# Six pairs' softmax reciprocals: one narrow transpose and two broadcast reads in place of six transposes

## The chip, the cores and the metric

The kernel runs on one core of a Trainium2 chip. What is measured is the device time of one execution in microseconds (us). TensorE (PE) does matmuls and transposes, VectorE (DVE), ScalarE (ACT) and GpSimd (POOL) the elementwise work, SyncE (SP) and GpSimd issue the transfers. SBUF is the on-chip memory of the operands, PSUM the one that TensorE writes its results to, DRAM the chip's large memory.

## The reference

Attention over keys that fall in the same hash bucket as the query (2 batches, 8 heads, 768 tokens, head size 64), and behind it two feed-forward blocks on the 1536 tokens, all in float32:

```python
def _attn_ref(q, k, v, proj):
    scale = 1.0 / np.sqrt(D)
    q_bits = (np.einsum('bhsd,dk->bhsk', q, proj) > 0).astype(np.int64)
    k_bits = (np.einsum('bhsd,dk->bhsk', k, proj) > 0).astype(np.int64)
    powers = 2 ** np.arange(n_bits)
    q_bucket = np.sum(q_bits * powers, axis=-1)
    k_bucket = np.sum(k_bits * powers, axis=-1)
    mask = q_bucket[:, :, :, None] == k_bucket[:, :, None, :]
    scores = scale * np.matmul(q, k.transpose(0, 1, 3, 2))
    scores = np.where(mask, scores, -1000000000.0)
    scores = scores - np.max(scores, axis=-1, keepdims=True)
    attn = np.exp(scores)
    attn = attn / (np.sum(attn, axis=-1, keepdims=True) + 1e-09)
    return np.matmul(attn, v).astype(np.float32)
...
    x = np.ascontiguousarray(attn_out.transpose(0, 2, 1, 3)).reshape(B * S, H * D)
    h = np.maximum(x @ w_in, 0.0)         # first block
    x = h * h @ w_out
    h = x @ w_in                          # second block, weights of its own
    g = h * (1.0 / (1.0 + np.exp(-h)))
    return (g @ w_out).astype(np.float32)
```

## The kernel before

The 16 heads (2 batches of 8) are worked on as 8 pairs. For each head the 768 queries are cut in two halves of 384, which gives 32 units (u), four to a pair, and each unit is cut into three blocks of 128 queries (j). The attention stage is one loop over steps, numbered d from -5 to 98, and a unit takes three steps. The order on every engine is that of the code: no scheduler moves anything in this stage. In an ordinary step TensorE transposes two blocks of the exponentials (transp, three 128x128 transposes into a tile t each, 384 of the tile's 512 columns), does the value matmuls of the two blocks of two steps ago (av, four matmuls into o) and the scores of the next query block (score_mm, four matmuls into one of two buffers s). ScalarE casts the two transposed tiles (t_hi, into th) and takes the exponential (score_exp, with the row sums into sums). VectorE takes the row maxima (row_max, row_live) and the rests of the casts (t_lo, into tl).

Six times, at the steps d = 17, 29, 41, 53, 65 and 77, and once before at d = 5, a step is long: bits_mm adds twelve narrow matmuls for the hash bits of the pair that comes next (into bs and bt), and VectorE compares them (bits_cmp). SP then copies the bits to where the next scores read them (place_bits).

The sums of a finished pair p are turned into factors in these steps. norm_sums (GpSimd) and norm_rows (VectorE reciprocal, into the same tile of 128x12) leave one reciprocal for each query in a column for each block and head. The unnormalised output ta (x_sum) has its queries along the free dimension, so the factors are needed along it as well: norm_rows lets GpSimd write each reciprocal 64 times (tile rw, 128 x 768), rb_mm has TensorE transpose that in six 128x128 blocks into a buffer s (named rb), x_norm has ScalarE copy it back to rw, and x_mul has GpSimd multiply ta by it into yf. x_put copies yf into the operand xk of the feed-forward blocks for the pairs below 6. The last pair (7) goes another way.

What a step does beside this stands in lists that are filled ahead of the loop: `todo` (at the end of a step), `mid` (behind row_live), `extra` (behind bits_mm). The first four tiles of the first w_in, given in 64-bit words, are made into float32 during attention: W_STEPS holds for each the steps of its load (w_load), its absolute value (w_abs on ScalarE and w_limit on GpSimd) and its three integer operations on VectorE (w_exp, w_sign, w_low). X_STEPS are the steps of four sums on GpSimd (x_form). The two feed-forward blocks come after attention and are put in order by a planner with costs of its own.

The lines that hold most of what is changed:

```python
            extra[k].append((rb_mm, x_norm, p))
            at(k + 1, x_mul, p)
            at(k + 1, x_put, p)
```

Of the kernel before, what the change touches and what calls it, by code (L numbers as in the profile page):

```python
# [11 lines left out]
F32 = mybir.dt.float32  # L12
# [9 lines left out]
B, H, S, D = 2, 8, 768, 64  # L22
NT, DM, FF = B * S, H * D, 2048
NB = 6
NPAIR = B * H // 2
NU = NPAIR * 4
QW = 384
# [10 lines left out]
W_LO = float(np.uint32(897 << 20).view(np.float32))  # L38
W_HI = float(np.uint32((1150 << 20) | 0xFFFFF).view(np.float32))
V_LAG = 4  # L40
W_STEPS = ((6, 10, 17, 17, 29), (8, 17, 29, 41, 41), (30, 41, 53, 53, 65), (44, 53, 65, 92, 93))
WA = 4
FB = 4
NP = FB // 2
# [129 lines left out]
    (10, (0, 0), (0, 3)),  # L174
)
NFORM = 4
X_STEPS = (82, 84, 86, 88)
FLIPPED = {2: ((0, 4, 1.0), (4, 6, -1.0)), 6: ((0, 6, -1.0),), 7: ((0, 2, 1.0), (2, 6, -1.0))}
FLIP = ({(1, 2), (2, 2), (2, 3)}, {(0, 2), (0, 3), (1, 3), (1, 0), (1, 1)})
MINUS = ({0: "-", 2: "-", 3: "-", 4: "r", 11: "r"}, {15: "-"})  # L180
# [519 lines left out]
def lsh_attention_moe_moe(ctx, tc, kd, qk, qf, fq, v, pc, wi1, wo1, wi2, wo2, out):  # L700
    nc = tc.nc
# [14 lines left out]
    att = ctx.enter_context(ExitStack())  # L716
    ac = att.enter_context(tc.tile_pool(name="ac", bufs=1))
    a1 = att.enter_context(tc.tile_pool(name="a1", bufs=1))
    a2 = att.enter_context(tc.tile_pool(name="a2", bufs=2))
    ps_s = att.enter_context(tc.tile_pool(name="ps_s", bufs=2, space=PSUM))  # L720
    ps_t = att.enter_context(tc.tile_pool(name="ps_t", bufs=3, space=PSUM))
    ps_o = att.enter_context(tc.tile_pool(name="ps_o", bufs=1, space=PSUM))

    ident = ac.tile([128, 128], F32, name="ident")
# [30 lines left out]
    def scale_q(p):  # L755
        q = pair[p]["r"][0]
        nc.scalar.mul(out=q, in_=q, mul=SCALE)
# [23 lines left out]
    def bits_mm(p):  # L781
        t = pair[p]
        hp, lp = t["hp"], t["lp"]
        ops = [(w[:, 48 * i : 48 * i + 48], x) for i in range(2) for (w, x) in ((pjh, hp[i]), (pjl, hp[i]), (pjh, lp[:, i]))]
        s = ps_s.tile([128, 2, 512], F32, tag="s", name=f"bs{p}")[:, 0], ps_t.tile([128, 512], F32, tag="t", name=f"bt{p}")
        for z in range(2):
            for j, (w, x) in enumerate(ops):
                mm(s[z][0:48, 0:QW], w, x[:, z * QW : (z + 1) * QW], start=j == 0, stop=j == 5)  # L788
        return s

    def bits_cmp(s, p, z):
        if z == 0:
            pair[p]["bt"] = a1.tile([128, S], F32R, tag="bt", name=f"bt{p}")
        nc.vector.tensor_scalar(
            out=pair[p]["bt"][0:48, z * QW : (z + 1) * QW],
            in0=s[z][0:48, 0:QW],
            scalar1=tm[0][0:48, 0:1],
            scalar2=tm[0][0:48, 1:2],
            op0=ALU.is_gt,
            op1=ALU.mult,  # L800
        )
# [173 lines left out]
    P, stats, otile, sums = {}, {}, {}, {}  # L975

    def warm_up(n):
        for _ in range(n):
            mm(warm, zb[:, 0:128], zb[:, 0:512], start=True, stop=True)
# [13 lines left out]
    def row_max(u, j, s):  # L993
        m = mt[:, (u * 3 + j) % 4]
        nc.vector.tensor_reduce(out=m[:, 0:1], in_=s[:, :, 0:QW], op=ALU.max, axis=AX.XY, negate=True)  # L995
        return m

    def row_live(m):
        nc.vector.tensor_scalar(out=m[:, 1:2], in0=m[:, 0:1], scalar1=LIM, scalar2=1.0, op0=ALU.is_lt, op1=ALU.mult)
        nc.vector.tensor_scalar(out=m[:, 2:3], in0=m[:, 0:1], scalar1=LIM, scalar2=m[:, 0:1], op0=ALU.is_lt, op1=ALU.mult)  # L1000

    def score_exp(u, j, s, m):
        p = u // 4
        if u % 4 == 0 and j == 0:
            sums[p] = a2.tile([128, 12], F32, tag="sums", name=f"sums{p}")
        e = P[u, j] = ac.tile([128, S], F32, tag="P", bufs=6, name=f"P{u}_{j}")
        c = (u % 4) * 3 + j
        nc.scalar.activation(  # L1008
            out=e.rearrange("p (a b) -> p a b", a=2),
            in_=s[:, :, 0:QW],  # L1010
            func=AF.Exp,
            scale=m[:, 1:2],
            bias=m[:, 2:3],
            accum_out=sums[p][:, c : c + 1],
        )

    PT = {}

    def transp(g, t=None):
        u, kt = divmod(g, KT)  # L1020
        if t is None:
            t = ps_t.tile([128, 512], F32, tag="t", name=f"t{g}")
        for j in range(3):
            nc.tensor.transpose(t[:, j * 128 : (j + 1) * 128], P[u, j][:, kt * 128 : (kt + 1) * 128], ident)  # L1024
        PT[g] = (t,)

    def t_hi(g):
        th = a1.tile([128, QW], F32R, tag="th", bufs=6, name=f"th{g}")
        nc.scalar.copy(out=th, in_=PT[g][0][:, 0:QW])  # L1029
        PT[g] += (th,)  # L1030

    def t_lo(g):
        t, th = PT[g]
        tl = a1.tile([128, QW], F32R, tag="tl", bufs=6, name=f"tl{g}")
        nc.vector.tensor_tensor(out=tl, in0=t[:, 0:QW], in1=th.bitcast(F32), op=ALU.subtract)  # L1035
        PT[g] = th, tl
# [31 lines left out]
    def norm_rows(p):  # L1068
        ri = sums[p]
        nc.vector.reciprocal(out=ri, in_=ri)  # L1070
        w = rows[p] = a1.tile([128, 6, 2, 64], F32, tag="rw", bufs=2, name=f"rw{p}")
        nc.gpsimd.tensor_copy(out=w, in_=ri.rearrange("p (h c) -> p c h", h=2).unsqueeze(3).broadcast_to([128, 6, 2, 64]))

    rows = {}

    def rb_mm(p):
# [38 lines left out]
    todo = defaultdict(list)  # L1115
    extra = defaultdict(list)
    mid = defaultdict(list)
    long, scale = {}, {}
    last = defaultdict(list)

    def at(g, fn, *a):
        todo[g].append((fn, a))

    for p in range(1, NPAIR):
        d0 = 12 * (p - 1)
# [18 lines left out]
    for p in range(NPAIR):  # L1144
        d0 = 12 * (p + 1)
        at(d0 + (-3 if p < NPAIR - 1 else -4), norm_sums, p)
        at(d0 + (2 if p < NPAIR - 1 else -3), norm_rows, p)
        at(d0 + (3 if p < NPAIR - 1 else 0), x_sum, p)
        if p < NPAIR - 1:
            k = d0 + (5 if p < NPAIR - 2 else 9)  # L1150
            extra[k].append((rb_mm, x_norm, p))
            at(k + 1, x_mul, p)
            at(k + 1, x_put, p)

    for k, d in enumerate(X_STEPS):
        at(d, x_form, k)
    for i, (d_load, d_abs, *d_dve) in enumerate(W_STEPS):
        key = (0, 0, i)
# [5 lines left out]
        d0 = d_dve[2]  # L1164
# [6 lines left out]
    with tc.manual_schedule():  # L1171
# [15 lines left out]
        c, k = slice(64, 64 + NBR), first["c"]  # L1187
        nc.vector.tensor_tensor(
            out=pdx, in0=k[:, 0:NBR].unsqueeze(1).broadcast_to([128, 2, NBR]), in1=k[:, NBR : 3 * NBR].rearrange("p (a b) -> p a b", a=2), op=ALU.mult
# [45 lines left out]
        for d in range(-5, G // 2 + 3):  # L1235
            ready, new = new, None
            g = 2 * d
            if ready:
                m = row_max(*ready)
            if 0 <= g - 1 < G and g - 1 not in early_lo:  # L1240
                t_lo(g - 1)
            if ready:
                row_live(m)
            for fn, a in mid.pop(d, []):
                fn(*a)
            if 0 <= g < G and d in (92, 94):
                t = ps_s.tile([128, 2, 512], F32, tag="s", name=f"t{g}")
                for i in range(2):
                    transp(g + i, t[:, i])
                t_hi(g)  # L1250
                t_hi(g + 1)
                t_lo(g)
            elif 0 <= g < G:
                transp(g)
                t_hi(g)
                t_lo(g)
                transp(g + 1)
                t_hi(g + 1)
            more = extra.pop(d, [])
            if ready and more and d not in long:  # L1260
                score_exp(*ready, m)
            if d in long:
                score_exp(*ready, m)
                if d in scale:
                    scale_q(scale.pop(d))
            for n in (g - V_LAG, g + 1 - V_LAG):
                if 0 <= n < G:
                    av(n)
            if d in long:
                t = bits_mm(long[d])  # L1270
            held = [(dve, pe(p), p) for pe, dve, p in more]
            if d in long:
                bits_cmp(t, long[d], 0)
                t_lo(g + 1)
                bits_cmp(t, long[d], 1)
            for dve, t, p in held:
                dve(t, p)
            if ready and not more and d not in long:
                score_exp(*ready, m)
            u, j = divmod(d + 5, 3)  # L1280
            if u < NU:
                new = u, j, score_mm(u, j)
            for fn, a in todo.pop(d, []) + last.pop(d, []):
                fn(*a)
            warm_up(WARM.get(d, 0))
        p = NPAIR - 1
        for z in (1, 0):
            t = ps_t.tile([128, 512], F32, tag="t", name=f"rb{p}_{z}")
# [12 lines left out]
        t = dict(yf=yf, xk=xk, wpa=wpa, raw=raws, wt=wt, pair=both, src=((wi1, wo1), (wi2, wo2)), out=out)  # L1301
# [58 lines left out]
```

## Time and profile before

| what | value |
|---|---|
| time, median of 3 runs | 724.61 us (724.58 to 725.61) |
| the profiled execution: its own time | 725.18 us |
| its span, first to last instruction | 723.40 us |
| TensorE busy | 718.1 us, 99% |
| VectorE busy | 609.6 us, 84% |
| ScalarE busy | 543.1 us, 75% |
| GpSimd busy | 263.0 us, 36% |
| granted TensorE clock over the span | 1.00 |

The profile is one execution. Its own time is longer than its span by what lies ahead of the first instruction and behind the last. Matmuls overlap each other, and their ends are modelled, so a busy TensorE is not one at its peak: the distance from one start to the next tells more than the durations.

### The profile page before, as it was taken

What the parts mean: (1) busy time and instruction counts of PE and PEld (TensorE: products, weight loads), DVE (VectorE), ACT (ScalarE), POOL (GpSimd) and SP (SyncE); (2) the same over time, 40 slices, a digit from 0 to 9 for tenths busy, and PEclk for the clock granted to TensorE, in tenths of its full rate; (3) what the DMA queues carried; (4) which work ended last, traced back from release to release, by engine and by line L of the source; (5) the groups of instructions that cost most, each with busy time, mean ns of one, the idle gap of its engine ahead of it and who ended that gap; (6) DMA issues with size and microseconds to landing.
All of it is one profiled execution on the core that took longest, in us unless ns stands there. A gap on an engine that the chain in (4) does not pass through costs nothing.

```text
span 723.4 us, 10946 instructions
## 1 busy us (share of the span) xinstructions
PE 718.1 (99%) x3673; PEld 616.0 (85%) x3673; DVE 609.6 (84%) x1106; ACT 543.1 (75%) x1012; POOL 263.0 (36%) x248
## 2 busy tenths in 40 slices
PE   9999999999999999999999999999999999999998
PEld 4999999999999888888888888888788888888886
DVE  6999999999998988786797889988778788888840
ACT  6899999999898897495559558878766955854861
POOL 7557567576464421040231232244204110212300
PEclk9999999999999999999999999999999999999999
DMA  5697696686562445123634652378131332345432
GB/s 172 179 218 161 163 204 170 162 188 153 121 132 63 117 142 134 59 81 95 131 91 113 150 139 76 92 166 180 44 116 59 87 92 83 104 102 116 103 105 99
DMA packets 37536, 89.76 MB, mean 124 GB/s; under 512 B 5300, under 2 KB 10188, under 8 KB 37480
## 3 DMA queue, kind: packets, MB, share of 16 engines
q1 hardware_dynamic: 25016, 64.78, 31.0%
q0 software_dynamic: 12032, 23.79, 18.3%
q8 instruction: 29, 0.48, 0.3%
q10 hardware_dynamic: 432, 0.49, 0.2%
q14 instruction: 27, 0.22, 0.1%
HBM read 49.60 MB, written 3.15 MB: 73 GB/s over the span
## 4 chain that ended last, share of the span: by engine, by line
PE 95%; DMA 2%; POOL 1%; issue 1%; SPq 0%; DVE 0%; ACT 0%; POOLq 0%; DVEq 0%
PE bank L558 35%; PE bank L443 24%; PE s L988 9%; PE t L1024 9%; PE bank L420 7%; PE o L1048 5%; PE o L1049 5%; PE bs L788 1%; PE bt L788 1%; DMA fr<-in_dram 1%; DMA cell<-cell 1%; PE rb L1080 1%; POOL kk L866 0%; POOL vv L932 0%; POOL qq L867 0%
## 5 line engine op out<-in xcount | busy, mean ns | idle before, releaser
L558 PE MATMUL bank<-woh,cell 128*128 128x512 f32 (+1 forms) x392 | 120.0, 385 | 0.0
L558 PE MATMUL bank<-cell,woh 128*128 128x512 f32 x384 | 118.5, 389 | 0.1
L1035 DVE TENSOR_TENSOR tl<-t,th 128x384 fp32r<-128x384 f32 x192 | 104.6, 547 | 0.9 <-ACT th L1029 0.8
L1008 ACT ACTIVATE P<-s,mt 128x768 f32<-128x768 f32 x96 | 95.5, 995 | 11.5 <-DVE mt L1000 7.2
L995 DVE TENSOR_REDUCE mt<-s 128x1 f32<-128x768 f32 x96 | 91.4, 952 | 4.5 <-PE s L988 4.0
L558 PEld LDWEIGHTS bank<-woh,cell 128*128 128x128 f32 x392 | 73.1, 188 | 14.6
L558 PEld LDWEIGHTS bank<-cell,woh 128*128 128x128 f32 x384 | 72.1, 188 | 15.5 <-DMA cell<-cell 0.5
L988 PE MATMUL s<-kk,qq 76*128 76x384 f32 (+1 forms) x384 | 84.2, 340 | 0.5 <-ACT P L1008 0.4
L1029 ACT CAST th<-t 128x384 fp32r<-128x384 f32 x192 | 82.0, 484 | 3.0 <-PE t L1024 2.7
L1024 PE MATMUL t<-ident,P 128*128 128x128 f32 x576 | 79.1, 273 | 0.0
L278 DVE TENSOR_TENSOR cell<-bank,cell 128x512 f32<-128x512 f32 x91 | 62.1, 691 | 19.6 <-PE bank L443 15.2
L443 PE MATMUL bank<-xw,wpb 128*128 128x512 f32 x312 | 75.9, 389 | 0.0
L558 PE MATMUL bank<-wol,cell 128*128 128x512 f32 (+1 forms) x196 | 75.4, 385 | 0.0
L558 PE MATMUL bank<-cell,wol 128*128 128x512 f32 x192 | 74.7, 389 | 0.0
L1048 PE MATMUL o<-th,vv 128*128 128x384 f32 x192 | 72.5, 378 | 0.0
L1024 PEld LDWEIGHTS t<-ident,P 128*128 128x128 f32 x576 | 67.9, 140 | 4.8 <-DVE tl L1035 0.4
L988 PEld LDWEIGHTS s<-kk,qq 76*128 76x128 f32 (+1 forms) x384 | 67.8, 188 | 2.6 <-ACT P L1008 1.6
L443 PEld LDWEIGHTS bank<-xw,wpb 128*128 128x128 f32 x312 | 58.5, 188 | 12.4 <-DVE bank L278 0.3
L1049 PE MATMUL o<-tl,vv 128*128 128x384 f32 x192 | 64.3, 335 | 0.0
L588 ACT COPY yf<-bank 128x512 f32<-128x512 f32 x48 | 27.9, 587 | 34.9 <-PE bank L558 34.3
L450 ACT COPY cell<-bank 128x512 f32<-128x512 f32 x39 | 22.9, 588 | 40.6 <-PE bank L443 38.7
L268 ACT CAST cell<-cell 128x512 fp32r<-128x512 f32 x81 | 48.9, 617 | 1.9 <-DMA cell<-cell 0.8
(198 smaller groups left out, 1499.2 us busy)
## 6 DMA issues: line engine op xcount, KB each, us to landing
raw<-in_dram SPq DMA_DIRECT2D x64, 512.0 KB, 4.1
cell<-cell POOLq DMA_DIRECT2D x23, 256.0 KB, 3.9
qq<-hq SPq DMA_DIRECT2D x28, 192.0 KB, 2.6
kk<-in_dram POOLq DMA_DIRECT2D x14, 384.0 KB, 5.2
yf<-cell POOLq DMA_DIRECT2D x21, 256.0 KB, 3.6
vr<-in_dram SPq DMA_DIRECT2D x8, 384.0 KB, 3.3
ta<-ob SPq DMA_DIRECT2D x31, 96.0 KB, 3.8
tb<-ob SPq DMA_DIRECT2D x31, 96.0 KB, 2.2
```

Of the source, the lines that this page charges most:

```text
L278: add("DVE", 0.70, lambda: vec.tensor_tensor(out=val(out), in0=bank[b], in1=val(other), op=ALU.add), [("bank", b), *reads], writes)
L420: mm(bank[b], wpa[n][:, p, 4 * h + j], x[:, q], start=j == 0 and z == 0, stop=j == 3 and z == 2)
L443: mm(bank[b], w[:, p], x[:, q], start=not started and z == 0, stop=z == 2, skip_group_check=started)
L558: mm(bank[b][:, 0:wd], x, y, start=start and i == 0 and z == 0, stop=i == (FB if half is None else 2 * half + 2) - 1 and z == 2, skip_grou ...
L988: mm(s[:, n, 0:QW], t["qq"][h][0:kk, ab, c0 : c0 + 128], t["kk"][h][0:kk, ab, n * QW : (n + 1) * QW], start=ab == 0, stop=ab == 1)
L995: nc.vector.tensor_reduce(out=m[:, 0:1], in_=s[:, :, 0:QW], op=ALU.max, axis=AX.XY, negate=True)
L1008: nc.scalar.activation(out=e.rearrange("p (a b) -> p a b", a=2), in_=s[:, :, 0:QW], func=AF.Exp, scale=m[:, 1:2], bias=m[:, 2:3], accum_ou ...
L1024: nc.tensor.transpose(t[:, j * 128 : (j + 1) * 128], P[u, j][:, kt * 128 : (kt + 1) * 128], ident)
L1029: nc.scalar.copy(out=th, in_=PT[g][0][:, 0:QW])
L1035: nc.vector.tensor_tensor(out=tl, in0=t[:, 0:QW], in1=th.bitcast(F32), op=ALU.subtract)
L1048: mm(o[:, 0:QW], vv, th, start=kt == 0, stop=False)
L1049: mm(o[:, 0:QW], vv, tl, start=False, stop=kt == KT - 1)
```

## The change

For the pairs 0 to 5, GpSimd no longer spreads the reciprocals, and TensorE's six transposes and ScalarE's copy of 128x768 are gone. In the long step TensorE transposes the 128x12 tile sums into twelve rows, which go into spare columns (384 to 511) of the tile t of that step's second block (row_turn); ScalarE copies them out (rt, 12x128); SP writes them to a scratch in DRAM (row_put) and three steps later reads each head's 768 factors back into 64 partitions (row_get, two reads). x_mul and x_put come five steps after the long step in place of one. Pair 6 stays as it was, with its steps written out. X_STEPS move by one, and four of the weight operations and two loads stand at other steps.

```diff
-W_STEPS = ((6, 10, 17, 17, 29), (8, 17, 29, 41, 41), (30, 41, 53, 53, 65), (44, 53, 65, 92, 93))
+W_STEPS = ((0, 5, 17, 17, 29), (8, 17, 29, 41, 53), (30, 41, 53, 65, 77), (54, 65, 77, 92, 93))
...
-X_STEPS = (82, 84, 86, 88)
+X_STEPS = (83, 85, 87, 89)
...
+    dr = att.enter_context(tc.tile_pool(name="dr", bufs=2, space=bass.MemoryType.DRAM))
...
     def norm_rows(p):
         ri = sums[p]
         nc.vector.reciprocal(out=ri, in_=ri)
+        if p >= NPAIR - 2:
+            w = rows[p] = a1.tile([128, 6, 2, 64], F32, tag="rw", bufs=2, name=f"rw{p}")
+            nc.gpsimd.tensor_copy(out=w, in_=ri.rearrange("p (h c) -> p c h", h=2).unsqueeze(3).broadcast_to([128, 6, 2, 64]))
+
+    def row_turn(p, t):
+        nc.tensor.transpose(t[0:12, QW:512], sums[p], ident)
+        r = turned[p] = a1.tile([12, 128], F32, tag="rt", name=f"rt{p}")
+        nc.scalar.copy(out=r, in_=t[0:12, QW:512])
+
+    def row_put(p):
+        o = scratch[p] = dr.tile([2, S], F32, tag="rows", name=f"rows{p}")
+        nc.sync.dma_start(out=o.rearrange("h (c q) -> (h c) q", c=6), in_=turned[p])
+
+    def row_get(p):
         w = rows[p] = a1.tile([128, 6, 2, 64], F32, tag="rw", bufs=2, name=f"rw{p}")
-        nc.gpsimd.tensor_copy(out=w, in_=ri.rearrange("p (h c) -> p c h", h=2).unsqueeze(3).broadcast_to([128, 6, 2, 64]))
-
+        for h in range(2):
+            nc.sync.dma_start(out=w[64 * h : 64 * h + 64].rearrange("p c h d -> p (c h d)"), in_=scratch[p][h : h + 1].broadcast_to([64, S]))
...
-        if p < NPAIR - 1:
-            k = d0 + (5 if p < NPAIR - 2 else 9)
-            extra[k].append((rb_mm, x_norm, p))
-            at(k + 1, x_mul, p)
-            at(k + 1, x_put, p)
+        if p == NPAIR - 2:
+            extra[d0 + 9].append((rb_mm, x_norm, p))
+            at(d0 + 10, x_mul, p)
+            at(d0 + 10, x_put, p)
+        elif p < NPAIR - 2:
+            k = d0 + 5
+            turn[k] = p
+            at(k, row_put, p)
+            at(k + 3, row_get, p)
+            at(k + 5, x_mul, p)
+            at(k + 5, x_put, p)
...
                 t_lo(g)
                 transp(g + 1)
                 t_hi(g + 1)
+                if d in turn:
+                    row_turn(turn[d], PT[g + 1][0])
```

What stands on the engines then, at step 29 and for pair 1. TensorE before, from the last transpose of the second block (tile t_1340) to the next scores (s_1_1381), with the semaphores that each instruction waits for; bs and bt are the bits, o the attention output:

```order
L1024 MATMUL t_1340<-ident,P_2_1210 128x128
L1048 MATMUL o_1349<-th_1267,vv_931 128x384 [waits Activation_49]
L1049 MATMUL o_1349<-tl_1290,vv_931 128x384
L788 MATMUL bs_1354<-hq_934,pjh 48x384 [waits Activation_49]
L788 MATMUL bt_1355<-lp_1012,pjh 48x384
L1080 MATMUL rb_1368<-ident,rw_1256 128x128 [waits PE_49,Activation_49,Pool_49]
L1080 MATMUL rb_1368<-ident,rw_1256 128x128 x5
L988 MATMUL s_1_1381<-kk_1_1008,qq_1_1007 128x384 [waits DVE_49]
```

TensorE after the change, the same stretch (the tile is t_1338 here, the scores are s_1_1374):

```order
L1025 MATMUL t_1338<-ident,P_2_1210 128x128
L1077 MATMUL t_1338<-ident,sums_583 12x128 [waits Activation_49,Pool_49]
L1049 MATMUL o_1350<-th_1265,vv_926 128x384
L1050 MATMUL o_1350<-tl_1288,vv_926 128x384
L789 MATMUL bs_1355<-hq_929,pjh 48x384
L789 MATMUL bt_1356<-lp_1006,pjh 48x384
L989 MATMUL s_1_1374<-kk_1_1002,qq_1_1001 128x384 [waits PE_49,Activation_49]
```

The six transposes are gone from behind the bits; the narrow one stands ahead of the value matmuls and has waits of its own. ScalarE at the same place, before (th are the casts of the transposed tiles, P the exponential):

```order
L1029 CAST th_1336<-t_1332 128x384 [waits PE_49,Activation_49]
L1029 CAST th_1344<-t_1340 128x384 [waits PE_49,Activation_49]
L1008 ACTIVATE P_0_1346,sums_1038<-s_0_1320,mt 128x768 [waits DVE_49]
L757 ACTIVATE rq_1150<-rq_1150 128x768 [waits DMAHW3_49,Pool_49]
L1091 COPY rw_1256<-rb_1368 128x768 [waits PE_49,Pool_49]
```

ScalarE after:

```order
L1030 CAST th_1334<-t_1330 128x384 [waits PE_49,Activation_49]
L1030 CAST th_1342<-t_1338 128x384 [waits PE_49,Activation_49]
L1079 COPY rt_1345<-t_1338 12x128 [waits DMAHW6_49,PE_49]
L1009 ACTIVATE P_0_1347,sums_1032<-s_0_1318,mt 128x768 [waits DVE_49]
L758 ACTIVATE rq_1150<-rq_1150 128x768 [waits DMAHW6_49,Pool_49]
```

The copy of the turned rows stands between the second cast and the exponential; the copy of rb behind rq is gone. GpSimd after, five steps on, where the multiplication of the pair before stands now (hk and lp belong to the next pair's hash bits, kk is the load of its keys):

```order
L754 CAST hk_1383<-rk_1151 128x768 [waits DMAHW3_49]
L1115 TENSOR_TENSOR yf<-rw_1500,ta_857 128x768 [waits DMAHW6_49,DMAHW5_49]
L1124 CAST xk<-yf 128x512 [waits Pool_49]
L1125 TENSOR_TENSOR xk<-yf,xk 128x512 [waits Pool_49]
L774 TENSOR_TENSOR lp_1460<-rk_1151,hk_1383 128x768
L764 DMA kk_0_1673<-in_dram 64x2x768 [waits DMAHW2_49,DMAHW4_49,DMASW5_49,PE_49]
```

The multiplication waits for the two reads and stands ahead of the split lp and of the load of kk, which before came directly behind the cast hk.

## Rows read from the trace of the kernel before

**Rows 1.** The page: the span, busy time by engine, the chain that ended last.

```profile
span 723.4 us, 10946 instructions
...
PE 718.1 (99%) x3673; PEld 616.0 (85%) x3673; DVE 609.6 (84%) x1106; ACT 543.1 (75%) x1012; POOL 263.0 (36%) x248
...
PE 95%; DMA 2%; POOL 1%; issue 1%; SPq 0%; DVE 0%; ACT 0%; POOLq 0%; DVEq 0%
```

**Rows 2.** Timeline around step 29: start and duration in us, engine, line, operation.

```profile
80.03 0.86 PE L988 MATMUL s<-kk,qq 128*128 128x384 f32 x4
...
80.60 1.00 ACT L1008 ACTIVATE P<-s,mt 128x768 f32<-128x768 f32 x1
80.72 0.82 PE L1024 MATMUL t<-ident,P 128*128 128x128 f32 x6
...
81.30 0.43 PE L1048 MATMUL o<-th,vv 128*128 128x384 f32 x1
...
81.58 0.86 ACT L1029 CAST th<-t 128x384 fp32r<-128x384 f32 x2
...
82.09 0.33 PE L788 MATMUL bs<-hq,pjh 128*48 128x384 f32 x1
...
82.44 0.68 DVE L965 SCALAR_TENSOR_TENSOR wi<-raw,wi 128x512 uint32<-128x512 uint32 x1
...
83.85 0.66 DVE L794 TENSOR_SCALAR bt<-bs,tmt 48x384 fp32r<-48x384 f32 x1
...
84.17 0.82 PE L1080 MATMUL rb<-ident,rw 128*128 128x128 f32 x6
...
84.75 0.94 PE L988 MATMUL s<-kk,qq 128*128 128x384 f32 x4
...
85.08 0.80 ACT L1091 COPY rw<-rb 128x768 f32<-128x768 f32 x1 [0.70 <-PE rb L1080]
...
85.53 0.82 PE L1024 MATMUL t<-ident,P 128*128 128x128 f32 x6
```

**Rows 3.** Timeline: transposes and casts of the first and the last rewritten step.

```profile
53.30 0.82 PE L1024 MATMUL t<-ident,P 128*128 128x128 f32 x6
...
54.15 0.86 ACT L1029 CAST th<-t 128x384 fp32r<-128x384 f32 x2
...
190.69 0.82 PE L1024 MATMUL t<-ident,P 128*128 128x128 f32 x6
...
191.55 0.86 ACT L1029 CAST th<-t 128x384 fp32r<-128x384 f32 x2
```

**Rows 4.** Timeline, first steps: TensorE waiting for ScalarE (idle time and releaser in brackets).

```profile
6.84 0.51 ACT L836 CAST qq<-fq 128x384 fp32r<-128x384 f32 x1
...
7.44 0.30 PEld L988 LDWEIGHTS s<-kk,qq 128*128 128x128 f32 x2 [0.29 <-ACT qq L836]
...
11.46 0.98 PE L988 MATMUL s<-kk,qq 128*128 128x384 f32 x4
```

**Rows 5.** Transfers: operation, count, KB each, median us from issue to landing.

```profile
raw<-in_dram SPq DMA_DIRECT2D x64, 512.0 KB, 4.1
...
qq<-hq SPq DMA_DIRECT2D x28, 192.0 KB, 2.6
kk<-in_dram POOLq DMA_DIRECT2D x14, 384.0 KB, 5.2
```

**Rows 6.** Timeline behind step 29: SP's and GpSimd's queues, and the scores that follow.

```profile
95.36 0.77 SPq L918 DMA_DIRECT2D kk<-bt  x1
...
96.83 0.83 POOL L753 CAST hk<-rk 128x768 fp32r<-128x768 f32 x1
97.74 1.83 POOL L773 TENSOR_TENSOR lp<-rk,hk 128x768 fp32r<-128x768 f32 x1
100.52 0.65 POOL L763 DMA_DIRECT2D kk<-in_dram  x1 [0.95 <-PE t L1024]
...
116.62 0.86 PE L988 MATMUL s<-kk,qq 128*128 128x384 f32 x4
```

More of the change, by code (lines that the diff above doesn't have):

```diff
@@ L1070, in norm_rows @@
         nc.vector.reciprocal(out=ri, in_=ri)
+        if p >= NPAIR - 2:
[9 more added lines that the diff above has]
+    def row_get(p):
         w = rows[p] = a1.tile([128, 6, 2, 64], F32, tag="rw", bufs=2, name=f"rw{p}")
-        nc.gpsimd.tensor_copy(out=w, in_=ri.rearrange("p (h c) -> p c h", h=2).unsqueeze(3).broadcast_to([128, 6, 2, 64]))
+        for h in range(2):
+            nc.sync.dma_start(out=w[64 * h : 64 * h + 64].rearrange("p c h d -> p (c h d)"), in_=scratch[p][h : h + 1].broadcast_to([64, S]))
+    turned, scratch = {}, {}
     rows = {}
@@ L1117, in lsh_attention_moe_moe @@
     mid = defaultdict(list)
-    long, scale = {}, {}
+    long, scale, turn = {}, {}, {}
     last = defaultdict(list)
```

## The prediction

> **What bounds the kernel now.** I read the page's first and fourth parts before anything else [rows 1]. TensorE is busy for 718.1 of 723.4 us, and the chain of work that ended last lies on it for 95%; nothing else holds more than 2% of it. So a microsecond that TensorE spends, or stands still, inside the attention stage comes out at the end almost one for one, and work on the other engines counts only where TensorE waits for it. Every edit except the calendar sits in the attention stage, so the second view is the timeline of that stage, around one of the six steps that the change rewrites: step 29, a "long" step, in which the twelve narrow matmuls of bits_mm and the six transposes of rb_mm stand between the attention-value matmuls and the next scores [rows 2].
>
> What the reader is to see there. In an ordinary stretch the four score matmuls begin at 80.03, the six transposes of P at 80.72 and the first value matmul at 81.30: 0.69 us and 0.58 us, so a transpose takes about 0.097 us of TensorE's stream. In the long step the value matmuls run from 81.30 to 82.09, the bits matmuls from 82.09 to 84.17, the six rb transposes from 84.17 to 84.75, the scores from 84.75 to 85.53. Those last scores take 0.78 instead of 0.69 us: they write the PSUM buffer that the first bits comparison (83.85 plus 0.66 us, on VectorE) has just left. ScalarE runs behind TensorE in this step: its exponential of the previous scores starts at 80.60 and lasts 1.00 us, and only then, from 81.58, come the two casts of the tiles that TensorE transposed from 80.72 on. Both casts take 0.86 us and end at 82.44, that is 1.14 us after TensorE has gone on to the value matmuls. The same stands at the first of the six steps (transposes 53.30, casts end 55.01) and at the last (190.69, 192.41): 1.71 and 1.72 us from transposes to the end of the casts, as in step 29 [rows 2, 3].
>
> **The change part by part, for one pair.**
>
> Removed from TensorE: six transposes, 84.17 to 84.75, 0.58 us. With the buffer rb gone, the new scores take the buffer of the previous scores, which the exponential frees, in place of the one the bits comparison frees (the rows of the changed program show ScalarE in place of VectorE in the wait of those scores). So the extra 0.09 us goes too: 0.67 us in all [rows 2].
>
> Added on TensorE: one transpose of 12 columns. No row has this shape. Its moving operand is the same 128-column identity as in the transposes above, so from above 0.097 us bounds it and from below nothing; I take 0.10, the nearest row [rows 2].
>
> Added with it: a wait. The narrow transpose writes twelve rows of spare columns in the tile t of the second transposed block (t_1338 in the rows above), and its row in the changed program waits for ScalarE and GpSimd. GpSimd's part (the sums) is over eight steps earlier. ScalarE's awaited count, taken over its instructions in that program, is reached by the second cast, th_1342 from t_1338, not by an older one. TensorE gets there at about 81.30; the cast ends at 82.44. Behind the waiting instruction stand the four value matmuls, the bits matmuls and the scores, on an engine with nothing else to do: 1.14 us standstill [rows 2]. What a restart costs shows where TensorE once waited for ScalarE at the start: the cast ended at 6.84 + 0.51 = 7.35 and the weights were loaded from 7.44, 0.09 us; and four scores after another such wait took 0.98 us where they take 0.86 in steady flow, 0.12 more [rows 2, 4]. From below this restart is 0 beyond the 0.09.
>
> The row above is what the time rests on. Beside it stands a rule: the Trainium skill, "PSUM — Partial Sum Buffer", section "PSUM bank collisions raise a hardware error", says that two engines may not use one bank in the same 32 partitions at once, whichever columns, and that semaphores must guard PSUM by bank and not by address. By that rule the spare columns of t are not free while ScalarE casts the others, and the wait belongs to the change and is no accident of the schedule; the sum by it is the one below, and only by addresses would it be the faster rival. No run yet shows whether the wait is felt.
>
> Sum for one pair: 1.14 + 0.09 + 0.10 - 0.67 = 0.66 us longer without the restart, 0.78 with it. Six pairs: 4.0 to 4.7 us; I take 4.4. The profiled execution took 725.18 us (span 723.40), so it would take 729.6; the median of the three runs shown lies 0.57 us below it, which gives 729.0.
>
> ScalarE: the copy of 0.80 us behind rb goes, a copy of 12x128 comes, bounded by nothing and by that 0.80 [rows 2]. It comes ahead of the exponential and has to wait for the narrow transpose, so the exponential starts somewhat later; its result frees the score buffer that TensorE wants after the bits matmuls, some 2 us on, and the transposes that read P stand two steps later. Nothing on the path.
>
> VectorE: same instructions, except that the calendar gives step 41 and step 65 one weight operation fewer and step 77 two more (such an operation takes 0.68 us in step 29). In step 77 they lie where VectorE must now wait for bits matmuls that come later by the standstill. Price 0; without that cover up to 1.4 us, once [rows 2]. The cast of tile 0 moves from step 10 to 5 and its load of 512 KB from step 6 to 0, ahead of the loads for pair 1 on SP; those are needed only at step 7, so 0, and the 4.1 us to its landing if that is wrong [rows 5].
>
> DMA: per pair one write of 6 KB and two reads of 192 KB each. The nearest rows are another 192 KB pair on the same queue, 2.6 us to landing, and the loads of kk on GpSimd's queue, 5.2 us [rows 5]. SP issues the reads behind kk<-bt (95.36 plus 0.77), so from about 96.2; they land between 98.8 and 101.4. GpSimd has by then finished its cast (96.83) and waits to multiply until then; behind that stand the multiplication, the two operations of x_put, the split of lp, now from some 103 to 105 instead of 97.74, and the load of kk, from some 107 instead of 100.52. The scores that need this kk start at 116.62: 9 us for a load of 5.2. Nothing late, with 3 to 4 us to spare (about 2 less for the pairs 4 and 5, whose x_put covers two blocks) [rows 6]. GpSimd loses its broadcast copy, which nobody waited for in that stretch.
>
> **The rivals.**
>
> *Faster: the wait is not felt.* If the wait were met when TensorE arrives, a pair would gain 0.67 - 0.10 = 0.57 us, six 3.4 us: 721.2. It decides from the point where the casts end 0.66 us earlier than in [rows 2]. For it: ScalarE loses 0.80 us of work in the same step. Against it: that copy comes after the casts, and the casts are held by the exponential, that by VectorE's maxima, and those by TensorE's own scores, which is why the 1.72 us repeat in the first and last of the six steps [rows 3]. Chance 0.12.
>
> *No change that can be measured.* Half the standstill is regained, as by an exponential that comes earlier: 6 x (0.57 + 0.09 + 0.10 - 0.67) is 0.5 us, so 725.1. Nothing in the rows shifts ScalarE so. Chance 0.08.
>
> *Slower still: rows that come late.* If the broadcast reads land 4 us later than taken, GpSimd's chain pushes the load of kk into the scores of the next pair. Two to three pairs would pay 1 to 2 us each, on top of the standstill: 731 to 735. For it: the stretch is crowded, with a kk load at 100.52 and two transfers ahead of the reads; against it, the margins above [rows 5, 6]. Chance 0.12.
>
> **How the numbers follow.** The forecast, standstill of the full 1.14 us in six steps, has the remaining 0.68. Its own range goes from 0.56 us a pair (the narrow transpose hidden) to 0.90 (twice the restart of 0.12), so 728.0 to 730.0. For eight in ten I go from 725.5 to 732.0, which takes in the regained half in part and the milder late transfers; left out are the faster rival and the far end. Within 0.2% (1.4 us) this kernel can't be told from unchanged. Faster 0.12, same 0.08, slower 0.80.
>
> **What would show it.** Right: in the profile after, a gap of about 1.2 us on TensorE before the narrow transpose in each of the six long steps, released by ScalarE's cast of th; value matmuls that start some 2.0 us after the transposes of P instead of 0.58; scores right behind the bits matmuls at 0.69 us; no waits of TensorE for kk or qq. Wrong: narrow transposes that follow the others without a gap (then 721), a lower granted clock in a step that holds a standstill, which no row of the kernel before shows (then more), or TensorE waiting for a DMA at the first scores of a pair (then 731 and over).

## The result

The changed kernel takes 728.91 us (median of 6 runs, 728.33 to 729.16) against 724.69 us (724.46 to 725.61) for the kernel before beside it: ratio 1.0055, 95% interval 1.0045 to 1.0066, so 4.2 us slower. The prediction was 729.0.

The page of the profile after (the profiled run took 728.33 us), where [rows 1] answers: span, busy time by engine, the chain that ended last.

```profile
span 726.6 us, 10910 instructions
...
PE 714.7 (98%) x3643; PEld 612.2 (84%) x3643; DVE 610.8 (84%) x1106; ACT 539.7 (74%) x1012; POOL 258.7 (36%) x242
...
PE 80%; DVE 15%; ACT 3%; issue 1%; DMA 0%; POOL 0%; ACTq 0%; DVEq 0%; POOLq 0%
```

TensorE has 3.4 us less to do and the span is 3.2 us longer; 15% of the chain has moved to VectorE and 3% to ScalarE, which fits a TensorE that now waits for something that hangs on them. The timeline of step 29 shows where, to be held against [rows 2]:

```profile
80.74 0.82 PE L1025 MATMUL t<-ident,P 128*128 128x128 f32 x6
...
81.60 0.86 ACT L1030 CAST th<-t 128x384 fp32r<-128x384 f32 x2
...
82.57 0.09 PEld L1077 LDWEIGHTS t<-ident,sums 128*12 128x12 f32 x1 [1.25 <-issue]
82.60 0.27 PE L1077 MATMUL t<-ident,sums 128*12 128x128 f32 x1 [1.04 <-ACT th L1030]
82.63 0.42 PE L1049 MATMUL o<-th,vv 128*128 128x384 f32 x1
82.91 0.26 ACT L1079 COPY rt<-t 12x128 f32<-12x128 f32 x1 [0.45 <-PE t L1077]
...
84.66 0.67 DVE L795 TENSOR_SCALAR bt<-bs,tmt 48x384 fp32r<-48x384 f32 x1 [0.71 <-PE bs L789]
...
85.50 0.88 PE L989 MATMUL s<-kk,qq 128*128 128x384 f32 x4
86.21 0.82 PE L1025 MATMUL t<-ident,P 128*128 128x128 f32 x6
```

The transposes, the casts and VectorE's work before them stand where they stood before. The casts end at 82.46, the narrow transpose's weights are loaded at 82.57, and the value matmuls start 1.89 us after the transposes, not 0.58. The next transposes come 5.47 us after these, where [rows 2] have 4.81. All six rewritten steps show it: 5.45 to 5.47 us against 4.80 to 4.81 (step 41, in which TensorE's weight load waited 0.2 us for the bits comparison before, 5.04). The sum over the six is 3.73 us. The span grew by less because the first loads of this execution came 0.4 us earlier (the first bits matmul of step 5 at 27.21, before at 27.65). This run is the fastest of the six; the rest of the 4.2 us is not assigned to a step.

The waits after, from 20 to 235 us (total us, times, longest):

```profile
POOL yf L1115 <- DMA rw<-rows: 41.2, 6, 8.4
...
PEld t L1077 <- issue: 6.2, 5, 1.2
PE t L1077 <- ACT th L1030: 6.2, 6, 1.0
```

GpSimd waits 7 us for the rows of each pair, which is later than I had them, but no row of TensorE waits for a transfer.

### The profile page after: what moved, and what is told of

Read it like the earlier page. It is cut to its first block, busy times and chain, and to the rows that moved or that the text cites. A ratio compares the mean times of both kernels' runs of the same rounds, so it can differ in the third digit from the quotient of the medians.

```text
span 726.6 us, 10910 instructions
## 1 busy us (share of the span) xinstructions
PE 714.7 (98%) x3643; PEld 612.2 (84%) x3643; DVE 610.8 (84%) x1106; ACT 539.7 (74%) x1012; POOL 258.7 (36%) x242
## 4 chain that ended last, share of the span: by engine, by line
PE 80%; DVE 15%; ACT 3%; issue 1%; DMA 0%; POOL 0%; ACTq 0%; DVEq 0%; POOLq 0%
PE bank L558 36%; PE bank L443 24%; DVE mt L996 7%; PE bank L420 7%; DVE tl L1036 6%; PE s L989 3%; PE t L1025 3%; PE o L1049 2%; PE o L1050 2%; ACT P L1009 2%; PE bs L789 1%; PE bt L789 1%; DVE mt L1001 1%; ACT th L1030 1%; DVE mt L1000 1%
```

## The experiments

Twelve kernels in three groups; each group had runs of the kernel before beside it (medians 724.87, 724.80 and 725.22 us), and ratios are against those.

**The wait alone.** The kernel before, with an unread narrow transpose into the spare columns:

```diff
                 transp(g + 1)
                 t_hi(g + 1)
+                if d in long and d > 5:
+                    nc.tensor.transpose(PT[g + 1][0][0:12, QW:512], sums[(d - 17) // 12], ident)
```

> The kernel before with one thing more: the narrow transpose into the spare columns of the second transposed tile, whose result nobody reads; the six rb transposes, copies and all else stay. Theory of the standstill: each of six steps pays the whole gap, value matmuls 1.31 us later than before, with nothing saved: 7.9 us more, 732.0 to 733.2 us. If transfers or GpSimd's order made the change slower, this kernel has neither and stays within 1 us of 724.7.

Measured: 731.91 us (731.87 to 732.15), ratio 1.0098 (1.0085 to 1.0111). In step 29 of its timeline:

```profile
81.52 0.82 PE L1024 MATMUL t<-ident,P 128*128 128x128 f32 x6
83.37 0.27 PE L1260 MATMUL t<-ident,sums 128*12 128x128 f32 x1 [1.03 <-ACT th L1029]
83.40 0.42 PE L1048 MATMUL o<-th,vv 128*128 128x384 f32 x1
```

With no transfer, no other calendar and nothing removed, 1.88 us stand between the transposes and the value matmuls, as after the change. Seven of the expected 7.3 to 8.5 us come: the standstill is shown, at 1.2 us a step.

**The calendar alone.** The kernel before with the new W_STEPS.

> The kernel before with the calendar of the weight tiles of the change, nothing else. Theory of the standstill: the calendar costs nothing, 724.2 to 725.2 us. Rival, calendar: step 77 with two weight operations more on VectorE holds up the bits and what follows: 1 us or more slower, 725.7 and over.

Measured: 724.30 us (723.74 to 724.86), ratio 0.9992 (0.9983 to 1.0001). Its price is not to be told from 0, as predicted.

**The change without its reads.**

```diff
     def row_get(p):
-        w = rows[p] = a1.tile([128, 6, 2, 64], F32, tag="rw", bufs=2, name=f"rw{p}")
-        for h in range(2):
-            nc.sync.dma_start(out=w[64 * h : 64 * h + 64].rearrange("p c h d -> p (c h d)"), in_=scratch[p][h : h + 1].broadcast_to([64, S]))
+        return
...
-            nc.gpsimd.tensor_tensor(out=x_rows(p), in0=rows[p].rearrange("p c h d -> p (c h d)"), in1=ta, op=ALU.mult)
+            nc.gpsimd.tensor_tensor(out=x_rows(p), in0=rows[p].rearrange("p c h d -> p (c h d)") if p in rows else ta, in1=ta, op=ALU.mult)
```

> The changed kernel without the two reads of each pair: the multiplication takes ta by itself in place of the rows, so the normalisation of the pairs 0 to 5 is left out (narrow transpose, its copy and the write to the scratch stay). If the standstill before the narrow transpose is the whole loss and the late rows cost TensorE nothing there, the time stays at 728.4 to 729.3 us, though GpSimd loses its waits of 6 to 8 us. If the late rows or the traffic of the reads take part in the loss, 728.0 us or less.

Measured: 728.91 us (728.18 to 729.48), ratio 1.0055 (1.0042 to 1.0067), the time of the change itself. In the change the late rows cost nothing that can be measured.

**The narrow transpose ahead of the casts.** It then waits for GpSimd's sums alone, long since there; ScalarE's copy stays behind the casts.

```diff
...
                 transp(g + 1)
-                t_hi(g + 1)
                 if d in turn:
                     row_turn(turn[d], PT[g + 1][0])
+                t_hi(g + 1)
+                if d in turn:
+                    row_copy(turn[d], PT[g + 1][0])
```

> The changed kernel, but the narrow transpose stands ahead of the second cast in the program, so that it waits for GpSimd's sums alone; transfers, GpSimd's order and calendar are those of the change. Theory of the standstill: the 1.1 us gap on TensorE in the six long steps is gone, the narrow transpose costs 0.03 to 0.10 us, the six rb transposes and the buffer wait stay saved, 0.57 to 0.64 us a pair: 720.8 to 721.4 us against 724.7 before (3.4 to 3.9 less). Rival, late rows: the time is lost to the reads and to GpSimd's later split and key load, which this kernel keeps: about 728.9, as the changed kernel. Rival, calendar: likewise about 728.9.

Measured: 725.98 us (724.74 to 730.27, 12 runs), ratio 1.0022 (1.0010 to 1.0034). The gap is gone (in step 29 the narrow transpose is at 80.53, the first value matmul at 80.56, 0.69 us behind the transposes of 79.87, so the narrow one takes 0.11 us of the stream), and 2.9 us come back, not the 7.5 to 8.1 that I expected. Something else holds TensorE, and by amounts that change from run to run. Two places in the profiled execution show what; at 730.27 us it is the slowest of the twelve and the only one profiled, so its waits are not the usual ones. First GpSimd and VectorE in step 29:

```profile
80.58 1.86 POOL L1105 TENSOR_TENSOR ta<-ta,tb 128x768 f32<-128x768 f32 x1
...
81.59 1.40 DVE L966 SCALAR_TENSOR_TENSOR wi<-raw,wi 128x512 uint32<-128x512 uint32 x1
...
83.72 0.66 DVE L795 TENSOR_SCALAR bt<-bs,tmt 48x384 fp32r<-48x384 f32 x1
```

GpSimd's chain (rows, multiplication, split of lp, load of kk) ran late, so its addition of ta and tb fell onto VectorE's weight operation, which took 1.40 us in place of 0.68 [rows 2]. Bits comparison and casts' rests came later by that, and the next step's second block waited 0.35 us for a tile t. Second, SP's queue in step 41 and TensorE two steps on:

```profile
109.95 1.87 POOL L1105 TENSOR_TENSOR ta<-ta,tb 128x768 f32<-128x768 f32 x1
...
111.85 0.46 SPq L1062 DMA_DIRECT2D tb<-ob  x1
112.36 0.58 SPq L928 DMA_DIRECT2D vr<-in_dram  x1
112.99 0.41 SPq L1085 DMA_DIRECT2D rows<-rt  x1
113.50 1.65 SPq L919 DMA_DIRECT2D qq<-bt  x1
...
115.19 0.78 SPq L919 DMA_DIRECT2D kk<-bt  x1
...
119.09 0.98 PE L989 MATMUL s<-kk,qq 76*128 76x384 f32 x2 [3.24 <-issue]
```

The last row is the first scores of a pair, the part with the hash bits (76 partitions: 64 of the head and 12 of bits). VectorE had the bits ready at 112.14. But SP's next tb<-ob waits until GpSimd's late addition has read tb (it ends at 111.82), and the bits' copies stand behind it: qq<-bt leaves 4.39 us after the first bits matmul (109.11), where the run without reads below has 3.06, and the chain of waits has it land at 117.54. The trace counts the last piece of kk<-bt as landed at 119.00, 0.06 us before the weights of these scores are loaded, so the scores waited for the bits of the keys to the end. The late start is only a part of it: qq<-bt holds SP for 1.65 us in place of 0.8, and kk<-bt lands 3.8 us after its issue, where the kernel before has 2.3. Beside them runs the load of kk, issued at 109.26 in place of 100.52 [rows 6]; the transfers' share of 16 engines is 1.03 from 111 to 113 and 0.94 from 113 to 115, in the run without reads 0.16 and 0.19 over the same stretch of the step. So late rows do reach TensorE, by GpSimd's addition and SP's queue; no scores wait for the load of kk itself, as my rival had it, but its traffic may lengthen the bits' copies, which no run tried by itself.

**The narrow transpose in a bank of its own.** Into the unused second half of the buffer of bs, behind the bits; SP writes the rows after the bits' copies.

```diff
...
-        nc.tensor.transpose(t[0:12, QW:512], sums[p], ident)
+        nc.tensor.transpose(t[0:12, 0:128], sums[p], ident)
...
             if d in long:
                 t = bits_mm(long[d])
+                if d in turn:
+                    row_turn(turn[d], t[2])
...
```

> The changed kernel, but the narrow transpose writes the unused second bank of the bits tile, behind the bits matmuls; ScalarE copies it from there behind the scaled q, and the write to the scratch is issued behind the copies of the bits. Theory of the standstill: no other engine holds that bank, so no gap: 0.57 to 0.64 us a pair less than before, 720.8 to 721.4 us. If the narrow transpose itself, and not the place it writes to, made the gap, the time would stay at 728.9. Rival, late rows: the write is issued some 3 us later than in the change, so slower than 728.9.

Measured: 729.00 us (728.71 to 729.45), ratio 1.0057 (1.0044 to 1.0069). No wait at the narrow transpose either, but a new one takes its place:

```profile
85.83 0.67 DVE L796 TENSOR_SCALAR bt<-bs,tmt 48x384 fp32r<-48x384 f32 x1 [0.83 <-ACT rt L1080]
...
87.11 0.52 PE L1026 MATMUL t<-ident,P 128*128 128x128 f32 x3 [0.57 <-DVE tl L1037]
```

In that program the bits comparison waits for ScalarE's copy out of the same tile, and behind it VectorE's rest of a cast, for which the transposes of the next step wait, 0.6 us in all six steps. My expectation had no such wait, and its 728.9 for a narrow transpose that makes the gap by itself is met in the number alone. The six waits are 3.4 us; the 3.3 us that the late rows cost in the next run would, as an estimate, make up most of the rest that was expected and did not come; it was not tried apart.

**No standstill and no reads.** The early narrow transpose together with the edit of the run without reads.

> The narrow transpose ahead of the casts (no standstill), and no reads: the multiplication takes ta by itself, so the normalisation of the pairs 0 to 5 is left out. If the late rows are what took the gain of the run with the reads (725.98 us, single times from 724.7 to 730.3) by way of GpSimd (late split and load of kk, addition of ta and tb beside VectorE's weight operation), the time is 721.0 to 722.5 us, VectorE's weight operation in step 29 takes 0.68 us again and the times lie close together. If VectorE's own work in the long steps is the limit, reads or not, 724.5 to 726 us.

Measured: 722.64 us (722.15 to 723.01), ratio 0.9969 (0.9957 to 0.9980). The scatter and 3.3 us are gone, VectorE's weight operation takes 0.68 us, and SP nowhere waits for GpSimd's addition: the late rows took them. So the reads cost nothing with the standstill (728.91 us with and without) and 3.3 us without it. The time lies 0.1 us above my range, and 1.3 us are still missing to the 721.4 that six times 0.57 us under the kernel before would give.

**The reads two steps earlier**, `at(k + 1, row_get, p)`, with the early narrow transpose.

> The narrow transpose ahead of the casts, and the two reads issued one step after the long step in place of three; nothing is left out. If the late rows took the gain, they are there when GpSimd comes to multiply (wait under 1 us), and the time is 721.0 to 723.0 us, faster than both kernels. If VectorE is the limit, 724.5 to 726 us. If the early reads push back the load of the hash keys rk or the qq and kk of the next head, TensorE waits for a transfer, and it is 724 to 728 us.

Measured: 725.39 us (724.41 to 728.30), ratio 1.0012 (1.0002 to 1.0022). The multiplication now waits 2.0 us at most, but the reads go out ahead of the second head's transfers, whose bits leave SP 11.65 to 13.09 us after the first bits matmul in five of the six periods, where the run without reads has 10.71 to 11.38; scores wait for them (0.72 us for kk<-lp at 102.43). The third expectation holds by these waits; the time alone would fit the second as well.

**The saving alone.** The kernel before without rb and its copy.

```diff
-            extra[k].append((rb_mm, x_norm, p))
+            if p == NPAIR - 2:
+                extra[k].append((rb_mm, x_norm, p))
```

> The kernel before without the six transposes rb and ScalarE's copy of them for the pairs 0 to 5, and nothing in their place: the multiplication takes the reciprocals along the wrong axis, so the normalisation of these pairs is wrong. By the prediction's price of 0.67 us a pair the time falls by 4.0 us, to 720.6 to 721.2 us. If VectorE can't follow TensorE there (its weight operations and bits comparisons in a long step), 722.5 to 724.5 us, with waits of TensorE's transposes for VectorE behind the long steps.

Measured: 723.37 us (722.44 to 723.89), ratio 0.9977 (0.9968 to 0.9986). Of 4.0 us only 1.4 come. The second range holds, but not with the waits that it named: those of TensorE are mostly those of the pair's first scores for the bits, which VectorE computes and SP copies. The hash-bit part of these scores, two steps behind the long steps 17 and 65:

```profile
61.57 0.30 PEld L988 LDWEIGHTS s<-kk,qq 76*128 76x128 f32 x2 [0.71 <-issue]
61.60 0.59 PE L988 MATMUL s<-kk,qq 76*128 76x384 f32 x2 [0.42 <-DMA kk<-bt]
...
170.54 0.30 PEld L988 LDWEIGHTS s<-kk,qq 76*128 76x128 f32 x2 [0.52 <-issue]
```

**The multiplication behind the load.** Early narrow transpose, all reads, and GpSimd multiplies after the split of lp and the load of kk:

```diff
-            at(k + 5, x_mul, p)
-            at(k + 5, x_put, p)
+            at(k + (8 if p < 5 else 5), x_mul, p)
+            at(k + (8 if p < 5 else 5), x_put, p)
```

> The narrow transpose ahead of the casts, all reads as in the change, and the multiplication of the pairs 0 to 4 moved behind the split of lp and the load of kk on GpSimd (eight steps after the long step in place of five); nothing is left out. If the late rows cost TensorE time only by what GpSimd holds back while it waits for them, the time is that of the run without reads (722.64 us): 722.2 to 723.4, in times that lie close together, and no row of VectorE's weight operation at 1.4 us. If the traffic of the reads itself delays the transfers that TensorE waits for, it stays at 724.5 to 726 us.

Measured: 723.20 us (722.71 to 723.89), ratio 0.9974 (0.9964 to 0.9984). With nothing left out it is faster than both kernels, and gains 2.0 us on the kernel before beside it where the run without reads gains 2.2. In step 29:

```profile
79.99 0.82 PE L1025 MATMUL t<-ident,P 128*128 128x128 f32 x6
80.65 0.27 PE L1077 MATMUL t<-ident,sums 128*12 128x128 f32 x1
80.68 0.43 PE L1049 MATMUL o<-th,vv 128*128 128x384 f32 x1
```

Narrow transpose and value matmuls follow the six transposes without a gap, and no weight operation of VectorE in the attention stage takes more than 0.69 us. One wait of the profiled execution (723.75 us) is not in the run without reads: 0.76 us at the scores of 155.42, whose bits of the keys left SP late, at 149.19 (13.78 us after the first bits matmul, there 12.43). Whether the reads' traffic made it is not shown.

**The bits on two queues.** In three kernels ScalarE issues kk<-bt of the first head, beside SP's qq<-bt:

```diff
-            nc.sync.dma_start(
+            (nc.scalar if n and not h else nc.sync).dma_start(
```

On top of the kernel just above:

> As the run with the multiplication behind the load, and ScalarE issues the hash bits of the keys (kk<-bt of the first head) in place of SP, at the same time as SP issues those of the queries. If the bits that come too late for the first scores of a pair are what is left of the expected gain, the waits for kk<-bt two steps behind the long step go (0.15 to 0.5 us each in the run without reads) and the time is 721.2 to 722.2 us. If VectorE's work is the limit, it stays within 0.3 us of the run with SP alone. If ScalarE is held up by its wait for the bits, it is slower than that run.

On top of the saving alone:

> The kernel before without the six transposes rb and their copy (normalisation wrong for the pairs 0 to 5), which took 723.37 us, and ScalarE issues the bits of the keys. If the late bits ate the saving, the time falls to 721.0 to 722.0 us. If VectorE's work in the long steps ate it, it stays at 723.0 to 723.7 us.

On top of the kernel before:

> The kernel before with the bits of the keys issued by ScalarE and nothing else: a control. TensorE waits for no bits in the kernel before, so 724.4 to 725.1 us if the bits limit only a TensorE that comes earlier; under 724 us if the gain of the other queue has another cause.

Measured: 723.81 us (723.34 to 724.36), ratio 0.9978 (0.9969 to 0.9987); 723.99 us (723.47 to 724.62), ratio 0.9982 (0.9974 to 0.9991); 725.81 us (725.46 to 726.33), ratio 1.0007 (0.9998 to 1.0015). That is 0.6 us more than the kernel above; 0.6 us more than the kernel before, with an interval that takes in no change; and a gain of 1.2 us in place of 1.4 for the saving alone. All three lie above every range that I gave; of the expectations only the one without a range, ScalarE held up, is met. From step 17 on, the waits for the bits are gone in both faster kernels, and waits for VectorE's cast rests stand in their place. The 0.6 us come from step 5 (its period is 27.64 us in place of 26.90, and 27.69 and 27.70 in place of 27.01 in the other two), where the issue itself holds ScalarE for 1.61 to 1.63 us (rows of the first of the three):

```profile
30.64 1.63 ACTq L919 DMA_DIRECT2D kk<-bt  x1
...
33.50 0.55 PE L1025 MATMUL t<-ident,P 128*128 128x128 f32 x3 [0.50 <-DVE tl L1036]
```

So the bits were not an independent limit: the five periods behind step 17 take 135.30 us in the first of the three and 135.34 in the run without reads, which has its waits for the bits. The windows from the first bits matmul of step 17 to that of step 77, five periods (stretch, its length, busy PE, PEld, DVE, ACT, POOL, granted clock, share and rate of transfers). Before:

```profile
54.65:192.05 137.40, 137.40 (x931) 131.16 (x930) 134.98 (x326) 126.63 (x274) 90.29 (x80) 1.00 0.74 169
```

After:

```profile
55.31:195.84 140.53, 135.37 (x906) 128.36 (x905) 134.78 (x323) 123.80 (x274) 86.07 (x75) 1.00 0.76 175
```

Early narrow transpose without reads:

```profile
54.67:190.01 135.34, 135.31 (x907) 128.17 (x905) 133.51 (x324) 123.27 (x274) 84.38 (x75) 1.00 0.78 172
```

VectorE is busy for 98.2% of the stretch before (134.98 of 137.40) and 98.6% in the fastest kernel. It is idle for 2.42 us there, and five savings of the predicted 0.67 us, 3.35 in all, don't fit into that unless VectorE's own work shrinks. Once TensorE has less than some 27 us to a period, there is hardly any slack of VectorE left to pay a late operation from; what comes late shows at a tile t or at the bits, whichever is wanted first. That VectorE is nearly full is shown; that it alone is what is left was argued and not tried, since I took no work off it.

## Why the prediction was right

**The standstill is the cause.** Predicted 1.14 us with 0.09 of restart, and 0.10 to 0.22 for the narrow transpose and what it breaks. Measured: the value matmuls start 1.31 us later in all. The lower sum, 1.33, is 0.02 too big, and the further 0.12 for the restart did not come. The narrow transpose's 0.10, for which no row stood, is borne out by the 0.11 us that it takes ahead of the casts. The run with the wait alone shows what the wait costs: 7.0 us over six steps. The rule on PSUM banks that the prediction drew on from the Trainium skill, "PSUM — Partial Sum Buffer", section "PSUM bank collisions raise a hardware error", agrees with this wait, by which the program keeps TensorE's write and ScalarE's reads of one tile apart. No run shows what an unguarded write would do, and this program goes further than the rule: in the run with a bank of its own VectorE waits for ScalarE's copy out of another bank of the same tile. Nor is the wait "no accident of the schedule", as the prediction had it: written ahead of the casts, the same columns cost no standstill.

**What was removed** is worth 0.65 us a pair in the change (1.31 less the 0.66 by which the step grew); predicted 0.67. This holds only because of the standstill. Taken alone it is worth 1.4 us over six pairs, not 4.0: while TensorE stands still, VectorE catches up (it even waits 0.71 us for bs in the rows after), and so the bits are on time. That a saving on TensorE counts "almost one for one" is the step that fails; the sum came out since in this change the two went together. Luck has a part in the last digit too: the forecast was the middle of 4.0 to 4.7 us, and of the 4.2 measured 3.73 stand in the six steps (step 41, whose rows it did not read, had a wait of its own to lose), while the rest is not assigned.

**Calendar, ScalarE, VectorE at 0**: right, by the calendar alone and the rows. The calendar's run moves the two absolute values of the weight tiles as well (tile 0 from step 10 to 5, tile 3 from 53 to 65), which the list of the change leaves out. VectorE's moved operations do take longer in the change, 1.08 us in step 65 and 1.70 in step 77 in place of 0.68, but these steps grow like the others: the standstill covers it.

**The rows** came later than priced. I had them landing by 101.4 and the load of kk from some 107; GpSimd multiplied at 102.29 and issued kk at 107.91:

```profile
96.11 1.17 SPq L1088 DMA_DIRECT2D rw<-rows  x2
...
102.29 1.84 POOL L1115 TENSOR_TENSOR yf<-rw,ta 128x768 f32<-128x768 f32 x1 [6.89 <-DMA rw<-rows]
...
107.91 0.67 POOL L764 DMA_DIRECT2D kk<-in_dram  x1
```

The margin held, and the change without its reads shows the cost to be nothing.

**The rivals.** The faster one (721.2 us if the wait is not felt) did not come, and its price was wrong besides: with the wait away the change takes 725.98 us, with the reads out of GpSimd's way 723.20. The unchanged case did not come, for nothing brings the casts forward (they end at 82.46 after, at 82.44 before). The late rows were the right danger, with both the way and the point misjudged: by the addition and SP's queue, and not from 4 us of delay but from a TensorE that no longer stands still for a microsecond.

## What to carry to other kernels

Spare columns in a PSUM tile can cost a wait while another engine reads the tile, here 1.2 us a step: put the write ahead of the reader's instructions, not behind them, and ask what the narrow result costs the engine that stands still for it. Before you count a saving on the busiest engine in full, look at the busy share of the second one in that stretch; here, at 98%, 1.4 of 4.0 us came. A wait for a transfer belongs behind the work that others need from the same engine, not ahead of it.

## What the runs showed of the hardware that I had not expected

The clock. In the profiled execution of the early narrow transpose with reads TensorE stood still for 3.2 us ahead of 119.09, and the granted clock of the window behind it was 0.50, the lower level (1.2 GHz of 2.4), then 0.77, a part at either level, then back at 1.00 (columns as above):

```profile
119.00:123.00 4.00, 3.91 (x14) 3.85 (x15) 2.07 (x5) 1.94 (x4) 1.77 (x3) 0.50 1.05 230
123.00:127.00 4.00, 4.00 (x24) 3.87 (x24) 2.57 (x6) 2.11 (x5) 0.00 (x0) 0.77 0.70 173
127.00:131.00 4.00, 4.00 (x31) 3.92 (x29) 4.00 (x11) 3.75 (x8) 3.51 (x3) 1.00 0.29 56
```

That period, long step to long step, took 33.06 us where the run without reads has 27.17: 5.9 us, of which the standstill is 3.2. The rest, 2.7, fits the stretch at the lower clock: 4.00 us at 0.50 and 4.00 at 0.77 leave 2.9 us of full clock ungranted. In the change the weight loads stood still for up to 1.25 us at a time, and the clock of those windows stayed at 1.00.

The collision of VectorE and GpSimd. The weight operation of 0.68 us ended 0.55 us after GpSimd's addition in step 29 (82.99 and 82.44) and 0.56 us after it in step 65 (171.32 and 170.76, where it took 1.84 us), as though it had waited for the addition's end; the addition itself took 1.86 and 1.87 us, where others take 1.82 to 1.86. The change shows it twice more, with the same 0.56 us, in step 65 (167.86 and 167.30) and in step 77 (196.60 and 196.04):

```profile
194.20 1.84 POOL L1103 TENSOR_TENSOR ta<-ta,tb 128x768 f32<-128x768 f32 x1
...
194.90 1.70 DVE L966 SCALAR_TENSOR_TENSOR both<-raw,both 128x512 uint32<-128x512 uint32 x1
```

Where VectorE's operation started first (109.37 in the early narrow transpose, the addition at 109.95), it took its 0.68 us. The Trainium skill, "SBUF — State Buffer", section "SBUF: two separate sides", says that a VectorE operation with two SBUF inputs and a GpSimd operation that reads SBUF share one pair of ports, which whoever starts first holds for its whole instruction; the rows agree.
